# An attention and MLP kernel: a reordered prologue, warm-up matmuls, and unread matmuls in PE gaps

## The chip, the cores and the metric

The kernel runs on one core of one Trainium2 chip. The time is the device time of an execution in microseconds (us), lower is better. Three numbers recur: the *time* of an execution, the *span* of its profile (from the first to the last instruction, about 1.9 us shorter than the time), and the *ratio* to the kernel before.

Engines: PE is TensorE (PEld its weight loads), DVE is VectorE, ACT is ScalarE, POOL is GpSimd, SP is the engine that issues most of the DMAs. Lines of the profile name a source line as L640; L640 in the kernel before and L711 in the changed one are the same statement, an exponential on ScalarE.

## The reference

```python
xn = layernorm(A_x)                         # [1, 2048, 512]
# A: attention with 32 heads of 16 columns
qkv = xn @ wqkv
p = softmax(q @ k.T * 16**-0.5)             # 32 heads x 2048 x 2048
attn = (p @ v) @ wo
# B: a token-mixing MLP
h = layernorm(xn)
u = gelu(einsum("bsd,sf->bdf", h, w1) + b1) # F = 1376
mix = (einsum("bdf,fs->bds", u, w2) + b2).T
out = xn_input + attn + mix                 # xn_input is A_x
```

The heavy part is the softmax: 32 x 2048 x 2048 exponentials.

## The kernel before

A score tile has 128 keys, two heads and 512 queries, so it fills 128x1024 elements of PSUM. There are 1024 such tiles, in 32 blocks of 32. Each tile's exponential is done either by one ScalarE instruction or by VectorE with an integer approximation and three shifted copies. PE then multiplies the result with V ("pv").

```python
def score_specs(n):                       # two matmuls on two 32-row groups of the array
    ...
    fn=lambda e: e.matmul(bank(bk), lhsT=KT[32*r:32*r+32, T, 128*kt:128*(kt+1)],
                          rhs=QT[32*r:32*r+32, b % 4, :], start=True, stop=True,
                          tile_position=(32*r, 0)),
    reads=[("KTt", T, kt), ("QT", b % 4, r)], writes=[("bank", bk)]
def exp_specs(n):                         # ScalarE
    fn=lambda e: e.activation(buf(pbuf[n]), ps[:, s_*1024:(s_+1)*1024], ACTF.Exp, scale=LN2_128)
def dexp_spec(n, w):                      # the same tile on VectorE
    fn=lambda e: e.tensor_scalar(buf_i(w), ps[:, s_*1024:(s_+1)*1024], IBIAS, 0.0, ALU.add, ALU.max)
```

The program has three parts. In the *head*, x is loaded, four tiles of 128 tokens are normalised, transposed and projected to K, Q and V. In *block 0*, 32 score tiles are all done on ScalarE in a fixed order, while the remaining twelve token tiles are prepared in between. From block 1 on, a list scheduler inside the kernel orders everything by a cost model of its own while the program is built: the order is static, the semaphores come from declared reads and writes.

Each pair of blocks gets its Q rows by eight small copies on the DMA queue, and a score may be scheduled only when its Q block is marked as available:

```python
def score_has(n):
    b, kt, qb, G, T, e_ = blk_of(n)
    return ("q", b - b % 2) in have and ("k", T, kt // 4) in have
def task_qt(qb, T):
    ...                                   # project, scale, then eight row copies
    for e_ in range(2):
        slot = (8 * qb + 2 * T + e_) % 4
        for r in range(4):
            a = 32 * r + 16 * e_
            yield "sp", [dict(dst=QT[a:a+16, slot, :], src=Qall[a:a+16, :], ...)]
    yield "call", lambda: have.add(("q", 8 * qb + 2 * T))   # after all eight
```

A MLP or projection task (`cur_ext`) holds one PSUM bank, `EX_BANK`, for its accumulation.

The softmax here doesn't subtract the row's maximum and nothing guards it: scores larger than these inputs give would overflow.

## Time and profile before

| | before |
|---|---|
| time | 736.1 us, median of 3 (734.94 to 736.33) |
| first exponential on ScalarE starts | 15.69 us |
| last exponential ends | 726.50 us |
| exponentials on ScalarE / VectorE | 758 / 266 |
| ScalarE's waits on scores from 20 us on | 7.0 us |

The first useful view is the page's busy table (part 1), here of the kernel before:

```profile
span 734.8 us, 28211 instructions
PE 686.5 (93%) x12384; PEld 305.5 (42%) x12384; DVE 637.7 (87%) x1060; ACT 709.5 (97%) x780; POOL 350.1 (48%) x390
```

The second is the chain that ended last (part 4), by engine:

```profile
ACT 77%; PE 15%; DVE 4%; DMA 1%; POOL 1%; issue 0%; SPq 0%; DVEq 0%
```

Both say ScalarE. So the span is best read along ScalarE as three stretches: the *head* until the first exponential, the *body* from there to the end of the last one, and the *tail*. Only what shortens one of these moves the time.

Where does the body lose time? The next view is the timeline of ScalarE alone. Columns: start, length, engine, line, operation, shapes, count of merged instructions, and in brackets the idle time before them with what ended it. The lines shown are those with a bracket, from 15 to 51 us and from 505 to 508 us in the kernel before:

```profile
15.69 5.74 ACT L640 ACTIVATE pT<-ps 128x1024 bf16<-128x1024 f32 x6 [0.32 <-PE ps L616]
22.79 1.94 ACT L640 ACTIVATE pT<-ps 128x1024 bf16<-128x1024 f32 x2 [1.35 <-PE ps L616]
25.27 22.85 ACT L640 ACTIVATE pT<-ps 128x1024 bf16<-128x1024 f32 x24 [0.55 <-PE ps L616]
48.36 1.02 ACT L640 ACTIVATE x_sb<-ps 128x1024 bf16<-128x1024 f32 x1 [0.24 <-PE ps L616]
50.22 1.02 ACT L640 ACTIVATE x_sb<-ps 128x1024 bf16<-128x1024 f32 x1 [0.83 <-PE ps L616]
...
505.17 1.02 ACT L640 ACTIVATE pT<-ps 128x1024 bf16<-128x1024 f32 x1 [0.67 <-PE ps L616]
506.52 1.02 ACT L640 ACTIVATE pT<-ps 128x1024 bf16<-128x1024 f32 x1 [0.32 <-PE ps L616]
507.93 4.69 ACT L640 ACTIVATE pT<-ps 128x1024 bf16<-128x1024 f32 x5 [0.39 <-PE ps L616]
```

Every wait shown is for a score matmul (L616). The windows view says why PE was late there. Columns: stretch, its length, then busy time and instruction count of PE, PEld, DVE, ACT and POOL, then the granted clock of TensorE (1.00 is full speed), the DMA share and GB/s:

```profile
18.00:26.00 8.00, 7.28 (x68) 3.69 (x67) 5.96 (x19) 6.10 (x7) 3.27 (x8) 0.58 0.46 111
46.00:50.00 4.00, 3.65 (x32) 0.91 (x32) 1.49 (x2) 3.15 (x4) 3.80 (x3) 0.57 0.00 0
497.00:508.00 11.00, 9.92 (x110) 3.34 (x114) 8.95 (x16) 9.06 (x11) 5.23 (x5) 0.53 0.06 11
541.00:549.00 8.00, 6.95 (x76) 2.25 (x76) 7.13 (x12) 6.96 (x9) 4.18 (x4) 0.57 0.03 5
655.00:663.00 8.00, 7.26 (x96) 2.53 (x94) 6.40 (x9) 7.58 (x9) 3.13 (x3) 0.79 0.18 47
```

These are the stretches of halved clock. By the clock records of this trace they last 6.83, 3.41, 10.24, 6.83 and 3.41 us. ScalarE (the fourth pair of numbers) loses 0.4 to 1.9 us in each. The mean clock of the profile is 0.979.

### The profile page before, as it was taken

The numbers are of one execution on the slowest core, as the hardware profiler recorded it, in microseconds if no ns is written. First come the engines' busy times: TensorE is split into PE (matmuls) and PEld (weight loads), VectorE is DVE, ScalarE is ACT, GpSimd is POOL, SyncE is SP. The second block draws the span as 40 slices with busy tenths as digits, with TensorE's granted clock in tenths as the row PEclk, the third lists the DMA queues.
The fourth block names the chain that finished last, engine by engine and source line by source line (L and its number), as shares of the span: only waits on it lengthen the run. The fifth ranks groups of instructions, "written<-read, shape, count | busy, mean of one in ns | idle before, by whom it ended". The sixth has DMA issues, their size and how long they took to land.

```text
span 734.8 us, 28211 instructions
## 1 busy us (share of the span) xinstructions
PE 686.5 (93%) x12384; PEld 305.5 (42%) x12384; DVE 637.7 (87%) x1060; ACT 709.5 (97%) x780; POOL 350.1 (48%) x390
## 2 busy tenths in 40 slices
PE   4989999999999999999889999989989999999997
PEld 3434445444444444433334443433434444434442
DVE  6857788888898888898989999898999899989887
ACT  4899999999999999999999999998999999999995
POOL 5448455432433334445454544544555545645443
PEclk9899999999999999999999999997989999999999
DMA  7401000124232222220000212110000221221201
GB/s 201 94 2 25 18 9 21 25 59 89 44 70 62 41 66 59 57 49 18 22 21 20 52 37 67 38 32 12 20 17 18 49 49 39 50 50 41 46 22 44
DMA packets 85691, 32.25 MB, mean 44 GB/s; under 512 B 67392, under 2 KB 85568, under 8 KB 85568
## 3 DMA queue, kind: packets, MB, share of 16 engines
q1 hardware_dynamic: 82256, 28.74, 17.2%
q8 instruction: 97, 1.59, 0.9%
q10 hardware_dynamic: 3312, 1.70, 0.8%
q14 instruction: 26, 0.21, 0.1%
HBM read 21.76 MB, written 2.35 MB: 33 GB/s over the span
## 4 chain that ended last, share of the span: by engine, by line
ACT 77%; PE 15%; DVE 4%; DMA 1%; POOL 1%; issue 0%; SPq 0%; DVEq 0%
ACT pT L640 56%; ACT x_sb L640 21%; PE ps L616 5%; PE ps L679 5%; PE ps L709 4%; DVE pT L651 1%; DMA x_sb<-in_A_x_dram 1%; DMA wblk<-in_B_w_dram 1%; DVE pT L656 0%; DVE stats L452 0%; ACT ga_sb L812 0%; DVE x_sb L651 0%; POOL hx L478 0%; DVE x_sb L656 0%; DVE V L767 0%
## 5 line engine op out<-in xcount | busy, mean ns | idle before, releaser
L640 ACT ACTIVATE pT<-ps 128x1024 bf16<-128x1024 f32 x539 | 537.7, 1178 | 5.3 <-PE ps L616 5.1
L616 PE MATMUL ps<-QT,KT 32*128 32x512 bf16 x2048 | 285.3, 391 | 21.0 <-ACT pT L640 10.3
L651 DVE TENSOR_SCALAR pT<-ps 128x1024 int16<-128x1024 f32 x192 | 234.1, 1219 | 37.9 <-PE ps L616 36.9
L679 PE MATMUL ps<-pT,V 128*32 128x256 bf16 x4464 | 246.9, 281 | 6.1 <-DVE V L767 1.8
L640 ACT ACTIVATE x_sb<-ps 128x1024 bf16<-128x1024 f32 x219 | 240.9, 1171 | 2.3 <-PE ps L616 2.2
L656 POOL TENSOR_SCALAR pT<-pT 128x1024 int16<-128x1024 int16 x141 | 147.5, 1046 | 154.8 <-DVE pT L656 100.5
L616 PEld LDWEIGHTS ps<-QT,KT 32*128 32x128 bf16 x2048 | 79.2, 91 | 198.8 <-ACT pT L640 92.1
L679 PEld LDWEIGHTS ps<-pT,V 128*32 128x32 bf16 x4464 | 104.4, 96 | 110.3 <-issue 80.7
L679 PE MATMUL ps<-x_sb,V 128*32 128x256 bf16 x1760 | 115.3, 279 | 4.1 <-DVE OT L870 1.7
L656 DVE TENSOR_SCALAR pT<-pT 128x1024 int16<-128x1024 int16 x270 | 113.9, 443 | 2.7
L651 DVE TENSOR_SCALAR x_sb<-ps 128x1024 int16<-128x1024 f32 x74 | 90.1, 1218 | 12.4 <-PE ps L616 12.1
L656 POOL TENSOR_SCALAR x_sb<-pT 128x1024 int16<-128x1024 int16 x55 | 57.5, 1046 | 84.2 <-DVE pT L656 56.7
L656 POOL TENSOR_SCALAR pT<-x_sb 128x1024 int16<-128x1024 int16 x57 | 59.6, 1046 | 60.3 <-DVE pT L656 46.7
L679 PEld LDWEIGHTS ps<-x_sb,V 128*32 128x32 bf16 x1760 | 45.1, 96 | 41.8 <-issue 25.0
L679 PE MATMUL ps<-pT,VM 128*32 128x256 bf16 x764 | 55.2, 278 | 0.3 <-POOL VM L531 0.3
L709 PE MATMUL ps<-hx,wblk 128*32 128x512 bf16 x688 | 53.7, 381 | 1.5 <-DVE Qall L731 0.8
L656 DVE TENSOR_SCALAR x_sb<-pT 128x1024 int16<-128x1024 int16 x110 | 48.6, 446 | 1.1
L656 DVE TENSOR_SCALAR pT<-x_sb 128x1024 int16<-128x1024 int16 x108 | 43.9, 434 | 1.1
L709 PE MATMUL ps<-wkv_raw,wblk 128*32 128x512 bf16 x512 | 43.0, 381 | 1.8 <-DMA wblk<-in_B_w_dram 1.2
L907 POOL TENSOR_TENSOR oT<-oC,denb 128x256 bf16<-128x256 f32 (+1 forms) x32 | 23.3, 728 | 27.9 <-DVE pT L656 14.5
L679 PEld LDWEIGHTS ps<-pT,VM 128*32 128x32 bf16 x764 | 20.5, 97 | 9.0 <-issue 2.7
L656 POOL TENSOR_SCALAR x_sb<-x_sb 128x1024 int16<-128x1024 int16 x17 | 17.8, 1046 | 13.3 <-DVE pT L656 11.6
(89 smaller groups left out, 438.1 us busy)
## 6 DMA issues: line engine op xcount, KB each, us to landing
wblk<-in_B_w_dram SPq DMA_DIRECT2D x10, 512.0 KB, 4.6
wblk<-in_B_w_dram SPq DMA_DIRECT2D x16, 320.0 KB, 3.8
oC<-OT SPq DMA_DIRECT2D x248, 16.0 KB, 1.8
denb<-rden_scratch SPq DMA_DIRECT2D x124, 32.0 KB, 1.9
xr<-in_A_x_dram SPq DMA_DIRECT2D x16, 128.0 KB, 2.4
dcomp<-OT SPq DMA_DIRECT2D x124, 2.0 KB, 1.7
QT<-Qall SPq DMA_DIRECT2D x120, 16.0 KB, 1.8
out_dram<-osb SPq DMA_DIRECT2D x14, 128.0 KB, 1.9
```

The source lines that it names most:

```text
L616: specs.append(dict(eng="pe", fn=lambda e, r=r, bk=bk: e.matmul(bank(bk), lhsT=KT[32 * r:32 * r + 32, T, 128 * kt:128 * (kt + 1)], rhs=QT[ ...
L640: return [dict(eng="act", fn=lambda e: e.activation(buf(pbuf[n]), ps[:, s_ * 1024:(s_ + 1) * 1024], ACTF.Exp, scale=LN2_128), reads=[("ban ...
L651: return dict(eng="dve", fn=lambda e: e.tensor_scalar(buf_i(w), ps[:, s_ * 1024:(s_ + 1) * 1024], IBIAS, 0.0, ALU.add, ALU.max), reads=[(" ...
L656: return dict(eng=eng, fn=lambda e: e.tensor_scalar(buf_i(o), buf_i(w), float(SHIFTS[k]), 1.0, ALU.add, ALU.mult), reads=[("pT", w)], writ ...
L679: specs.append(dict(eng="pe", fn=lambda e, c=c, h=h, i=i, off=off: e.matmul(bank(PV_BANK)[32 * c:32 * c + 32, 256 * par:256 * par + 256], ...
L709: specs.append(dict(eng="pe", fn=lambda e, c=c, w=w: e.matmul(bank(EX_BANK)[32 * c:32 * c + w, :], lhsT=lhs_of(32 * c, 32 * c + w), rhs=rh ...
L907: yield "pool", [dict(eng="pool", fn=lambda e, cs=cs: e.tensor_tensor(oT[0:m, qb % 2, T, cs], oC32[0:m, tb_, cs], denb[0:m, tb_, cs], ALU. ...
```

## The change

Its intent: start the exponentials earlier, and keep TensorE's clock up, by matmuls whose results nobody reads. Four parts:

1. *Head*: x tiles 0 to 3 are loaded ahead of the weights on two queues; one tile's statistics go to ScalarE; the wo_t memset and the V projection leave the head; Q is evacuated in halves, V in pairs of tiles.
2. *Head warm-ups*: eleven matmuls of 512 columns before the first transpose.
3. *Block-0 warm-ups*: five at period 1, three each at periods 14 and 15.
4. *Fills*: from block 1 on, wherever the kernel's own model sees a gap of PE and little activity in the last 3.42 us, unread matmuls (the 3.42 us and the bound are constants chosen in the kernel, `ACT_WIN` and `ACT_MIN`).

Besides, many operations of the head get new cost figures in the scheduler's model.

The diff, cut to its core:

```diff
+N_WARM = 11
+ACT_WIN = 3.42
+ACT_MIN = 0.5
+    def pe_activity(self, t): ...        # modelled busy share of PE in the last ACT_WIN us
...
-        for j, a, b in (2,0,1),(1,0,1),(0,0,1),(1,1,4),(2,1,4),(0,1,4): ld_w on the ACT queue
-        ld_x(0, 1); ld_x(1, 2); ld_x(2, 4); ...                     # (shortened)
+        ld_x("sp", 0, 1); ld_x("act", 1, 2); ld_x("sp", 2, 3); ld_x("act", 3, 4)
+        for j in (1, 0, 2):
+            ld_w(j, 0, 1)
...
+        def warm_up(n, bk):
+            for _ in range(n):
+                sc.add("pe", lambda e: e.matmul(bank(bk), lhsT=warm[:, 0:128], rhs=warm, start=True, stop=True), ...)
+        ln_sums(1)
+        warm_up(N_WARM, 5)
...
+        for t in range(NPRE):
+            ln_norm(t)
+        late_memsets()                     # four memsets of VM on GpSimd
+        for t in range(NPRE):
+            transpose_pe(t, TB[t])
...
+            if period == 1:
+                warm_up(5, PV_BANK)
+            if period >= NKT - 2:
+                warm_up(3, 4)
...
+        def fill(t_next, same):
+            if cur_ext is not None or last_n is None or sc.pe_activity(t_next) > ACT_MIN:
+                return
+            ...
+            for _ in range(int((t_next - sc.pe_end - 2 * PE_SWITCH - 0.1) / 0.22)):
+                sc.add("pe", lambda e: e.matmul(bank(EX_BANK), lhsT=ident[:], rhs=wo_c[:, 0, :], ...), name="fill")
+            if kind in ("score", "pv", "ext"):
+                fill(t_est, kind == "score" and t_est <= sc.pe_end - 0.05)
```

## The prediction

5.3 + 2.5 + 2.8 = 10.6 us come off 736.1, which gives the 725.5.

> **What bounds the kernel now.** ScalarE. The page's busy table gives it 709.5 us of 734.8; the chain of waits that ended last is 77% ScalarE, nearly all exponentials. The groups view has 758 on ScalarE (539 + 219) and 266 on VectorE; back to back in the timeline, ScalarE starts one each 0.92 us, so 758 x 0.92 + 11 tanh x 0.5 is about 702 us that this change does not touch. The rest is a head of 15.7 us before the first exponential, about 8.5 us after the last, and idle time between (waits view from 20 us on: 7.0 us, all on score matmuls).
>
> Head (timeline): the first x tile's statistics are done at 3.97 us, but GpSimd is in a 1.8 us memset (wo_t) until 5.95, so its normalisation starts at 6.95; the third x tile lands only at 7.5, behind six weight loads on the other queue; PE runs at half speed until about 12.3 (0.61 us for four 128x128 matmuls, then 0.39).
>
> Idle time between (windows view): the granted clock is 0.50 in about 19.5-26, 46.5-50, 497-507.5, 541.5-548.5, and low around 655-662. ScalarE loses there 1.9, 1.1, 1.95, 1.1 and 0.3 us. [...] these stretches follow thin PE work (2-us windows with 6 to 10 matmuls at 496 and 540) and last multiples of about 3.4 us.
>
> **What changes.** Removed from the head: the wo_t memset, the V evacuations and half of the Q work before the first score; x tiles 0 to 3 now load ahead of the weights on two queues; one tile's sums go to ScalarE. Added: eleven 512-column warm-up matmuls (about 0.43 us each cold, 4.7 us, in idle time). Laid out with measured durations (statistics 0.69 + 0.18, power 0.57, normalise 0.4, transposes 0.4 warm, copy 0.6, evacuation 0.3 to 0.5): four normalised tiles at about 7.8 us, both Q halves and K tile 0 at about 9.9, first exponential at about 10.4. Gain 5.3 us, all on the chain (4 to 6.5).
>
> ScalarE stays the limit in block 0. Warm-ups at periods 1, 14 and 15 should save most of the 3.0 us lost around 20-26 and 46-50. I take 2.5.
>
> The unread matmuls land only in modelled gaps of over 0.5 us; I expect 100 to 400, PE busy up a little. They cost next to nothing: PE waits there for a score bank anyway. They save most of the 3.4 us lost around 500, 545 and 660: I take 2.8.
>
> The list schedule is computed anew, so the split of exponentials may move by a few either way: each is 0.92 us for ScalarE. I expect 755 to 761 on ScalarE; that is the widest term.
>
> **Prediction.** 736.1 - 5.3 - 2.5 - 2.8 = 725.5 or so: 725. Range 719 to 730. Faster by over 2% (below 721.4): 0.22; within 2%: 0.76; slower: 0.02.
>
> **Right or wrong would show as:** first exponential at 9.5 to 11.5 us in the timeline; no clock of 0.50 after the first exponential and a mean clock above 0.99; ScalarE's waits on scores from 20 us on below 2.5 us instead of 7.0; ScalarE busy total about the same within 4 us.
>
> **What would make it wrong:** weights landing late behind the x tiles, so that the first score waits for a DMA; fills that delay scores (a new wait on PE in full-array matmuls); clock drops that the model's activity does not see; VectorE falling behind in block 0; a different split.

## The result and the profile after

The median fell from 736.22 us (4 runs, 734.94 to 737.40) to 729.52 us (4 runs, 728.75 to 729.66): ratio 0.9907, 95% interval 0.9889 to 0.9925. The same changed kernel (the control e5 below) gave 730.20 and 0.9928. It was run at another time.

The page of the changed kernel, parts 1 and 4:

```profile
span 727.8 us, 28362 instructions
PE 690.1 (95%) x12448; PEld 307.5 (42%) x12459; DVE 636.5 (87%) x1060; ACT 706.9 (97%) x779; POOL 352.1 (48%) x390
ACT 70%; PE 20%; DVE 7%; POOL 1%; issue 1%; DMA 0%; DVEq 0%; ACTq 0%
```

ScalarE is as busy as before, within 2.6 us, but its share of the chain fell from 77% to 70% and PE's rose from 15% to 20%. Something on PE has become more of a limit than it was. ScalarE's timeline of the changed kernel, again the lines with a bracket from the first exponential to the last long wait, shows it:

```profile
11.25 3.77 ACT L711 ACTIVATE pT<-ps 128x1024 bf16<-128x1024 f32 x4 [0.48 <-PE ps L687]
15.40 26.87 ACT L711 ACTIVATE pT<-ps 128x1024 bf16<-128x1024 f32 x28 [0.38 <-PE ps L687]
245.18 1.02 ACT L711 ACTIVATE x_sb<-ps 128x1024 bf16<-128x1024 f32 x1 [0.53 <-PE ps L687]
256.95 1.02 ACT L711 ACTIVATE pT<-ps 128x1024 bf16<-128x1024 f32 x1 [0.20 <-PE ps L687]
258.51 1.02 ACT L711 ACTIVATE pT<-ps 128x1024 bf16<-128x1024 f32 x1 [0.53 <-PE ps L687]
302.87 3.77 ACT L711 ACTIVATE pT<-ps 128x1024 bf16<-128x1024 f32 x4 [3.75 <-PE ps L687]
```

The many waits around 22, 48, 505 and 545 us are gone. In their place stands one of 3.75 us at 302.87, longer than any wait for a score in the kernel before. Along ScalarE the profiles differ like this (the first two rows are read from the timeline, the tail is span minus the end of the last exponential):

| | before | after | difference |
|---|---|---|---|
| head: first exponential starts | 15.69 | 11.25 | -4.44 |
| body: first start to last end | 710.81 | 707.47 | -3.34 |
| tail | 8.30 | 9.08 | +0.78 |
| span | 734.8 | 727.8 | -7.0 |

The body's 3.34 us can be split further. One exponential fewer is on ScalarE (757 for 758), worth 0.92. The waits view from 20 us on has 5.2 us for 7.0: the old kinds of waits fell by about 5.5 us, from 7.0 to 1.5, and the new one put 3.75 back. The remaining 0.7 us is not in shorter waits: one of 0.38 us at 15.40 lies before the 20 us mark, and idle gaps under 0.15 us, which the view leaves out, rose from 0.3 to 0.6 us in all. It is in ScalarE's own busy time, which fell in the body from 703.5 to 701.2 us, 1.4 more than the one exponential explains. Counted in the trace, an exponential that starts after any idle time occupies ScalarE for 1.02 us, one that follows without a gap adds 0.92; there were 26 of the first kind and are 16. So each wait costs ScalarE about 0.1 us beyond its own length, here about 1.1 us together; the rest of the 1.4 is not traced further.

What was PE doing before 302.87? The chain in order of time (start, length, what) of the changed kernel:

```profile
298.71 2.08 PE ps L750 x76
300.78 1.73 PE ps L780 x32
302.51 0.54 PE ps L687 x6
```

PE was not idle and not slow. It worked through 76 pv matmuls and 32 of a projection (L780) before the next score (L687), because that is the program's order. The SP queue's timeline at the same place shows what the scheduler was holding the scores back for:

```profile
293.86 3.04 SPq L386 DMA_DIRECT2D QT<-Qall  x5
296.94 0.58 SPq L386 DMA_DIRECT2D denb<-rden_scratch  x1
297.57 2.03 SPq L386 DMA_DIRECT2D wblk<-in_B_w_dram  x2
...
301.76 2.73 SPq L386 DMA_DIRECT2D QT<-Qall  x3
```

Five of the eight row copies of a Q pair are issued at 293.86, then other transfers come in between, and the last three follow only at 301.76. The four that the waiting block needs are among the first five. But the scheduler releases the pair's scores only after the eighth.

### The profile page after: what moved, and what is told of

Its sections match the earlier page's. It is cut to its first block, busy times and chain, and to the rows that moved or that the text cites. A ratio compares the mean times of both kernels' runs of the same rounds, so it can differ in the third digit from the quotient of the medians.

```text
span 727.8 us, 28362 instructions
## 1 busy us (share of the span) xinstructions
PE 690.1 (95%) x12448; PEld 307.5 (42%) x12459; DVE 636.5 (87%) x1060; ACT 706.9 (97%) x779; POOL 352.1 (48%) x390
## 4 chain that ended last, share of the span: by engine, by line
ACT 70%; PE 20%; DVE 7%; POOL 1%; issue 1%; DMA 0%; DVEq 0%; ACTq 0%
ACT pT L711 50%; ACT x_sb L711 20%; PE ps L687 7%; PE ps L780 6%; PE ps L750 6%; DVE pT L722 3%; DVE pT L727 1%; DVE x_sb L722 1%; DVE x_sb L727 1%; DMA x_sb<-in_A_x_dram 0%; PE ps L595 0%; POOL pT L727 0%; ACT ga_sb L883 0%; PE ps L1030 0%; POOL mv L478 0%
## 5 line engine op out<-in xcount | busy, mean ns | idle before, releaser
L711 ACT ACTIVATE pT<-ps 128x1024 bf16<-128x1024 f32 x548 | 545.6, 1172 | 6.1 <-PE ps L687 5.6
L687 PE MATMUL ps<-QT,KT 32*128 32x512 bf16 x2048 | 283.8, 385 | 18.8 <-ACT pT L711 10.1
L722 DVE TENSOR_SCALAR pT<-ps 128x1024 int16<-128x1024 f32 x179 | 218.2, 1219 | 31.0 <-PE ps L687 30.2
L711 ACT ACTIVATE x_sb<-ps 128x1024 bf16<-128x1024 f32 x209 | 233.7, 1184 | 0.6 <-PE ps L687 0.5
L727 POOL TENSOR_SCALAR pT<-pT 128x1024 int16<-128x1024 int16 x133 | 138.9, 1045 | 145.7 <-DVE pT L727 97.8
L687 PEld LDWEIGHTS ps<-QT,KT 32*128 32x128 bf16 x2048 | 79.7, 91 | 192.8 <-ACT pT L711 83.8
L722 DVE TENSOR_SCALAR x_sb<-ps 128x1024 int16<-128x1024 f32 x88 | 107.4, 1220 | 16.8 <-PE ps L687 16.2
L727 DVE TENSOR_SCALAR pT<-pT 128x1024 int16<-128x1024 int16 x256 | 106.6, 442 | 2.2
L727 POOL TENSOR_SCALAR pT<-x_sb 128x1024 int16<-128x1024 int16 x63 | 65.8, 1045 | 70.0 <-DVE pT L727 57.8
L780 PE MATMUL ps<-hx,wblk 128*32 128x512 bf16 x688 | 54.9, 381 | 0.8 <-DVE u_sb L875 0.3
L727 DVE TENSOR_SCALAR pT<-x_sb 128x1024 int16<-128x1024 int16 x131 | 53.5, 437 | 1.3
L780 PE MATMUL ps<-wkv_raw,wblk 128*32 128x512 bf16 x512 | 43.8, 390 | 0.5 <-DVE osb L925 0.5
L727 DVE TENSOR_SCALAR x_sb<-pT 128x1024 int16<-128x1024 int16 x98 | 41.6, 436 | 0.8
L727 POOL TENSOR_SCALAR x_sb<-x_sb 128x1024 int16<-128x1024 int16 x25 | 26.1, 1045 | 31.4 <-DVE pT L727 21.3
L750 PEld LDWEIGHTS ps<-pT,VM 128*32 128x32 bf16 x796 | 21.1, 96 | 10.4 <-issue 4.5
```

What stands on the lines that cost most here:

```text
L687: specs.append(dict(eng="pe", fn=lambda e, r=r, bk=bk: e.matmul(bank(bk), lhsT=KT[32 * r:32 * r + 32, T, 128 * kt:128 * (kt + 1)], rhs=QT[ ...
L711: return [dict(eng="act", fn=lambda e: e.activation(buf(pbuf[n]), ps[:, s_ * 1024:(s_ + 1) * 1024], ACTF.Exp, scale=LN2_128), reads=[("ban ...
L722: return dict(eng="dve", fn=lambda e: e.tensor_scalar(buf_i(w), ps[:, s_ * 1024:(s_ + 1) * 1024], IBIAS, 0.0, ALU.add, ALU.max), reads=[(" ...
L727: return dict(eng=eng, fn=lambda e: e.tensor_scalar(buf_i(o), buf_i(w), float(SHIFTS[k]), 1.0, ALU.add, ALU.mult), reads=[("pT", w)], writ ...
L750: specs.append(dict(eng="pe", fn=lambda e, c=c, h=h, i=i, off=off: e.matmul(bank(PV_BANK)[32 * c:32 * c + 32, 256 * par:256 * par + 256], ...
L780: specs.append(dict(eng="pe", fn=lambda e, c=c, w=w: e.matmul(bank(EX_BANK)[32 * c:32 * c + w, :], lhsT=lhs_of(32 * c, 32 * c + w), rhs=rh ...
```

## The experiments

Two techniques keep the comparisons clean. The head and block 0 have a fixed order, so a change there shifts the rest without reordering it. And an unread matmul can be cut from 512 columns to 1 instead of being removed: order, semaphores and schedule stay the same, only its work is gone. The time that each kernel's own model gives is printed when it builds; it is used below only to say what was scheduled, not as a time. "Phase" means only whether the clock was first granted early or late in an execution.

| run | what | mean us | runs | ratio |
|---|---|---|---|---|
| after | the change | 729.36 | 4 | 0.9907 |
| e5_after_again | the change, control | 730.01 | 6 | 0.9928 |
| e1_qgate | + early release of Q blocks | 728.10 | 6 | 0.9902 |
| e2_fill1 | fills cut to 1 column | 732.47 | 6 | 0.9964 |
| e3_warmhead1 | head warm-ups cut to 1 column | 729.92 | 6 | 0.9929 |
| e4_warmbody1 | block-0 warm-ups cut to 1 column | 730.91 | 6 | 0.9943 |
| e6_h12 | two waits of the head removed | 729.40 | 6 | 0.9920 |
| e7_h3 | more head warm-ups | 728.07 | 5 | 0.9902 |
| e8_all | e1 + e6 + e7, no period-1 warm-ups | 725.78 | 5 | 0.9869 |
| e9_q3 | e1 + e7 | 726.05 | 5 | 0.9860 |
| e10_reorder | all unread matmuls cut to 1 column | 734.30 | 6 | 0.9972 |
| e11_beforefill | the kernel before + fills | 733.39 | 6 | 0.9961 |
| e12_all2b | e8, fills before a task starts, bound 0.55 | 726.18 | 5 | 0.9861 |

The runs e1 to e4 shared one chip, e5 to e8 a second, e9 to e12 a third; the runs of the kernel before, 11 in each, averaged 735.28, 735.36 and 736.28. All outputs were correct.

### e1_qgate: is the 3.75 us wait the lost gain?

My theory: the wait comes only from the release rule and costs its full length. Rival: PE has that work to do anyway and the wait moves.

```diff
-        return ("q", b - b % 2) in have and ...
+        return ("q", b) in have and ...
-            yield "call", lambda: have.add(("q", 8 * qb + 2 * T))         # after eight copies
+                yield "call", lambda e_=e_: have.add(("q", 8 * qb + 2 * T + e_))  # after each four
```

> The changed kernel, but a score may be scheduled as soon as the four row copies of its own Q block are queued, not all eight of the pair. My theory: the one new ScalarE wait of 3.75 us at 303 us comes only from the scheduler holding that block's scores back, so it vanishes and the time falls by 3 to 4 us, to about 726; 0.986 to 0.987 of the kernel before. Rival: the PE work at 299 to 303 us has to be done somewhere, and the wait only moves: within 1 us of 729.5 and other score waits of 3 us or more in its place.

Measured: 728.23 us median, 0.9902. The wait was gone from the profile, but the time fell by 1 to 2 us only, so on the time alone neither side was right. The profile showed where the rest went: the first exponential started at 12.62 instead of 11.25 us, with the same instructions in the head. One exponential more was on ScalarE (758), and a clock drop around 256 to 265 us took 1.7 us in waits. The body was 1.86 us shorter. The head's 1.4 us was a new question.

### e3_warmhead1 and e5_after_again: the head's warm-ups

```diff
         def warm_up(n, bk):
+            w = 1 if n == N_WARM else 512
             for _ in range(n):
-                ... e.matmul(bank(bk), lhsT=warm[:, 0:128], rhs=warm, start=True, stop=True)
+                ... e.matmul(bank(bk)[:, 0:w], lhsT=warm[:, 0:128], rhs=warm[:, 0:w], start=True, stop=True)
```

> The changed kernel in the same order, but the eleven warm-up matmuls ahead of the first transpose stream 1 column. Theory: the head's transposes and projections (about 54 matmuls of 128 columns between 6.7 and 10.8 us) then run at half speed for most of their length, and the first exponential starts 1 to 1.5 us later than 11.25; total 730.5 to 731. Rival: VectorE and GpSimd pace the head and PE only follows: first exponential within 0.3 us of 11.25 and the total unchanged.

> The changed kernel unaltered, as a control on the same chip as the next three. Theory: [...] in some executions the first exponential comes at 11.25 us, in others near 12.6, so the times should fall into groups about 1.4 us apart within 728.5 to 731. Rival: the spread is only noise of one group and the profile shows 11.25 again.

Without the warm-ups' work the first exponential came at 12.68 us, as my theory said. But the mean was 729.92 against 730.01 of the control: on average the eleven matmuls were worth nothing that shows above the noise (each is uncertain by about 0.4 us). The control's own profile has the first exponential at 12.51. PE's timeline of the head shows it; first the changed kernel as first profiled:

```profile
6.71 1.22 PE L526 MATMUL ps<-ident,hx 128*128 128x128 bf16 x12 [0.66 <-DVE hx L498]
8.54 0.40 PE L526 MATMUL ps<-ident,hx 128*128 128x128 bf16 x4 [0.61 <-DVE hx L498]
8.77 0.39 PE L577 MATMUL ps<-xnT,wq_sb 128*128 128x128 bf16 x4
9.22 0.83 PE L577 MATMUL ps<-xnT,wq_sb 128*128 128x128 bf16 x12
```

and the same kernel in the control:

```profile
1.17 4.26 PE L595 MATMUL ps<-osb 128*128 128x512 bf16 x11 [1.17 <-DVE b1c_bf L396]
6.77 1.21 PE L526 MATMUL ps<-ident,hx 128*128 128x128 bf16 x12 [1.34 <-DVE hx L498]
8.59 0.61 PE L526 MATMUL ps<-ident,hx 128*128 128x128 bf16 x4 [0.61 <-DVE hx L498]
8.99 0.63 PE L577 MATMUL ps<-xnT,wq_sb 128*128 128x128 bf16 x4
9.85 1.49 PE L577 MATMUL ps<-xnT,wq_sb 128*128 128x128 bf16 x12
```

Four transposes take 0.40 us in one and 0.61 in the other, twelve projections 0.83 and 1.49. In the control the clock was granted early: the eleven warm-ups took 4.26 us, while in the first profile they took 4.87. It was then withdrawn just ahead of the projections: the windows view gives the control a clock of 0.52 from 8 to 10 us and of 0.63 from 10 to 12, which is half speed from 8.1 to 11.5. (The windows view counts the time before the first clock record as 1.00, also where the durations say half speed: in e3 it reads 1.00 from 6 to 10 us, while four 128-column matmuls take 0.61 to 0.63 us there, against 0.39 to 0.40 in the first profile. So durations decide in the head.) The time of the first grant, read from the clock records, differs between the profiles. Three of the six profiles with eleven full warm-ups have the slow head: e5, e1 and e4, with the grant at 4.67, 4.89 and 4.89 us (their warm-ups took 4.26, 4.37 and 4.37 us) and a fall 3.4 us later, which lasted 3.4 us. In the three with the fast head (e6, the first profile, e2) the grant came at 5.11, 6.35 and 6.45 us (warm-ups of 4.48, 4.87 and 4.88 us) and nothing was withdrawn before 255 us. The slow head thus goes with an early grant in these six; why the grant comes earlier in one execution than in another is not shown. The expected groups are only partly visible in the control's times (727.94, then 730.10 to 731.10), because drops elsewhere overlap with them.

### e7_h3: warm-ups that hold

```diff
-N_WARM = 11
+N_WARM = 13
         for t in range(NPRE):
             transpose_pe(t, TB[t])
+            if t < NPRE - 1:
+                warm_up(1, 5)
```

> The changed kernel with 13 warm-ups instead of 11 and one more after each of the first three tiles' transposes. Theory: the clock no longer falls between the warm-ups and the projections in either phase, so no execution has its head matmuls at 0.61 to 0.63 us per four after 8.5 us: first exponential 11.3 to 11.9 in the profile, the slower group of executions disappears and the mean falls by 0.3 to 0.8 us. Rival: [...] the clock falls as before, and the extra warm-ups only delay: mean 0 to 0.8 us longer.

All five executions lay between 727.95 and 728.41 us and had a mean clock of 1.000, against 727.94 to 731.10 in the control. The mean fell by 1.94 us, more than expected, as no drop occurred in the body either. The drop at 256 us comes and goes as well. All twelve profiles of the changed kernel and its variants have one ScalarE wait of 0.53 us that ends between 244.7 and 248.5 us. In six of them the clock falls 10.3 to 11.0 us after its end (the changed kernel, e1, e2, e3, e5, e8); in the other six, e7 among them, it stays at 1.00 there. What decides between the two is not shown. So e7's five even executions may be in part luck: e9, with the same head, had a mean clock below 1.000 in three of five. PE's timeline of the head in e7:

```profile
6.69 0.40 PE L526 MATMUL ps<-ident,hx 128*128 128x128 bf16 x4 [0.29 <-DVE hx L498]
6.92 0.38 PE L595 MATMUL ps<-osb 128*128 128x512 bf16 x1
7.21 0.40 PE L526 MATMUL ps<-ident,hx 128*128 128x128 bf16 x4
7.45 0.38 PE L595 MATMUL ps<-osb 128*128 128x512 bf16 x1
...
9.23 0.83 PE L577 MATMUL ps<-xnT,wq_sb 128*128 128x128 bf16 x12
```

Its idle time before the first transpose is 0.29 us instead of the control's 1.34, and a warm-up matmul follows each of the first three tiles' transposes. None of the four profiles with this head (e7, e8, e9, e12) has slow projections (twelve take 0.83 us in e7 and e8), e9 included, where the grant came at 4.44 us by its clock record, earlier than in the three slow ones. In the control the clock fell across 16 transposes and two gaps (1.34 and 0.61 us); e7 put matmuls between the transposes and shortened the gaps to 0.29 and 0.28 us in one edit, so which of the two made the difference is not told apart here.

### e2_fill1: are the fills worth anything?

The changed kernel has 41 fills, all after 314 us. They were cut to 1 column.

```diff
-                    bank(EX_BANK), lhsT=KT[...], rhs=QT[32 * r:32 * r + 32, b % 4, :], ...
+                    bank(EX_BANK)[:, 0:1], lhsT=KT[...], rhs=QT[32 * r:32 * r + 32, b % 4, 0:1], ...
-                sc.add("pe", lambda e: e.matmul(bank(EX_BANK), lhsT=ident[:], rhs=wo_c[:, 0, :], ...
+                sc.add("pe", lambda e: e.matmul(bank(EX_BANK)[:, 0:1], lhsT=ident[:], rhs=wo_c[:, 0, 0:1], ...
```

> The changed kernel in the same instruction order, but the 41 unread matmuls of the fills stream 1 column instead of 512. Theory: the fills hold the clock up, so without their work two or three stretches of clock 0.50 return after 314 us, with 2 to 3.5 us of ScalarE waits on scores: about 732. Rival: the new schedule has no stretch thin enough, the 41 fills do nothing, and the time stays within 0.5 us of 729.5 with a clock of 1.00 after 314 us.

Measured: mean 732.47, ratio 0.9964 against 0.9928 for the control, about 2.5 us slower; and two executions of six ran slower still, up to 734.77 at a mean clock of 0.983. The windows view from 322 to 342 us, first e2:

```profile
322.00:342.00 20.00, 18.67 (x272) 7.80 (x272) 16.71 (x29) 18.06 (x21) 9.95 (x11) 0.74 0.06 15
```

then the changed kernel:

```profile
322.00:342.00 20.00, 18.63 (x313) 8.39 (x310) 18.02 (x31) 19.75 (x23) 10.98 (x12) 1.00 0.09 16
```

The clock is 0.74 in one and 1.00 in the other, and ScalarE works 18.06 us of 20 against 19.75. The order is the same, and the first grant came at about the same time (6.45 and 6.35 us), so this is the work of the unread matmuls and nothing else. The rival falls. But the place matters: this stretch, 327.3 to 337.5 us in the clock records, is none that the kernel before had. At its old places, around 500, 545 and 660 us, e2 keeps the full clock without the fills' work, for example:

```profile
500.00:510.00 10.00, 8.85 (x148) 3.50 (x144) 8.88 (x15) 10.00 (x12) 4.97 (x5) 1.00 0.09 24
540.00:550.00 10.00, 9.23 (x158) 4.18 (x158) 9.93 (x17) 10.00 (x13) 6.22 (x6) 1.00 0.13 26
```

e10's profile shows the same. In these executions the old stretches went with the new order of the program; whether a first grant at another time would bring them back is not shown. In three of e2's six the mean clock was lower (0.983 to 0.988) than in the profiled one (0.991); where those fell is not recorded.

### e4_warmbody1: the warm-ups of block 0

The same edit as in e3, for the groups of five and three.

> The changed kernel in the same order, but the warm-ups inside block 0 (five at period 1, three each at periods 14 and 15) stream 1 column. Theory: the five at period 1 delay a score by about 0.4 us, but without any of them the clock falls to 0.50 around 16 to 23 us or 42 to 46 us and ScalarE loses 1 to 3 us: 730.5 to 732. Rival: the block-0 warm-ups are not needed with the head's in place, no stretch of 0.50 appears before 50 us, and the time falls by 0.3 to 0.5 us to about 729.1.

Measured: mean 730.91, ratio 0.9943; against before it gains about 1.0 us less than the control, at the small end of my theory. In its profile the clock is 1.00 from 12 to 42 us and falls from 42 to 50 (0.61, 0.50, 0.50 and 0.68 in steps of 2 us), with waits of 0.49, 0.82 and 0.41 us; so the six at periods 14 and 15 are needed (e10's profile has the same stretch). The five at period 1 looked superfluous. That reading came from one profile, with its first grant at 4.89 us; e12 speaks against it.

### e6_h12: two waits of the head

In the changed kernel's timeline the fourth normalisation takes 0.87 us, and three GpSimd memsets run at the same moment:

```profile
7.61 0.87 DVE L498 TENSOR_SCALAR hx<-x_sb,mv 128x512 bf16<-128x512 bf16 x1
7.53 0.81 POOL L413 MEMSET VM<- 128x256 bf16 x3
```

The other three take 0.38 to 0.41. That the memsets hold up the fourth is my estimate from this coincidence, and e6 tests it by moving them. The second wait is one of bookkeeping: both halves of Q declare a write of the same key, so ScalarE's half waits 0.72 us for VectorE's.

```diff
-        late_memsets()                      # in the head
+            if period == 13:
+                late_memsets()
-        [("QT", 0, r) for r in range(4)]
+        [(("QT", 0, r) if half else ("QT0a", r)) for r in range(4)]
-        reads=[("KTt", T, kt), ("QT", b % 4, r)]
+        reads=[("KTt", T, kt), ("QT", b % 4, r)] + ([("QT0a", r)] if b == 0 else [])
```

> The changed kernel with two waits of the head taken away: GpSimd's four VM memsets moved from the head to period 13 of block 0, and the two halves of Q kept under separate keys so that ScalarE's half no longer waits for VectorE's. Nothing else in the order changes. Theory: the fourth normalisation takes 0.41 instead of 0.87 us [...], and the wait of 0.72 us before the ScalarE half of Q goes: first exponential 0.7 to 1.0 us earlier than the control at the same clock phase (about 10.4 where that has 11.25), total 0.7 to 1.0 us less. Rival: the K tiles' evacuation or the copies bind next and it gains under 0.3 us.

By the time it is inconclusive: mean 729.40 against 730.01, and both kernels have the lottery of the head's clock. The profile decides. The tile view of e6 (durations as minimum/median/maximum in ns):

```profile
L498 DVE TENSOR_SCALAR hx<-x_sb,mv x5: 380/407/414, 6.3 to 11.8; 128x512 bf16<-128x512 bf16 x5
```

No normalisation is slow any more (at most 0.414 us, with the memsets elsewhere), so the memsets beside it were the cause; by what mechanism is not shown. The first exponential starts at 10.74 us, 0.51 earlier than the 11.25 that the changed kernel has when its head runs at full speed. The only executions of this call with a mean clock of 1.000 differ by as much: 727.42 and 727.94; but one of the changed kernel in the first measurement took 728.75 at 1.000, so the times alone prove little. Expected were 0.7 to 1.0; ScalarE's half of Q now waits 0.52 us for the projections on PE, which bind next. What each of the two edits gave alone was not run.

### e9_q3: the first experiment without the lottery

The edits of e1 and e7 together.

> The changed kernel with the more robust head warm-ups (as in e7_h3) and the early release of Q blocks: the first experiment again, now without the lottery of the head's clock. Its schedule puts 758 exponentials on ScalarE against 757, so at equal waits it owes 0.9 us. Theory: against e7_h3 (728.0) the wait of 3.75 us goes and 0.9 us comes back: 725.2 to 725.8. Rival: the PE work of 299 to 303 us takes ScalarE's time elsewhere and the gain stays under 1 us: above 727.

Measured: 725.68 us median (724.97 to 727.14), ratio 0.9860. Against e7 in the profiles, at the same start of the first exponential (11.26), the body shrank from 706.22 to 703.50 us, by 2.7: 3.75 gained, 0.92 owed for the extra exponential, 2.8 expected. ScalarE's timeline of e9 at the old place:

```profile
295.79 2.08 ACT L713 ACTIVATE pT<-ps 128x1024 bf16<-128x1024 f32 x2
298.28 1.02 ACT L713 ACTIVATE pT<-ps 128x1024 bf16<-128x1024 f32 x1 [0.41 <-PE ps L689]
299.20 3.77 ACT L713 ACTIVATE x_sb<-ps 128x1024 bf16<-128x1024 f32 x4
302.81 2.90 ACT L713 ACTIVATE pT<-ps 128x1024 bf16<-128x1024 f32 x3
```

A wait of 0.41 us is left of 3.75, on a score that waits 0.18 us for one of its row copies. The rival of e1 falls: the work that PE did in the hole fits elsewhere. Two of its five executions had a mean clock of 0.995 and took about 727; the other three 725.0 to 725.7.

### e10_reorder: the order alone

The edits of e2, e3 and e4 together.

> The changed kernel in the same order with every unread matmul (warm-ups and fills) cut to 1 column: the new order of the head alone. Theory: the parts add: the fills were worth about 2.7 us, the warm-ups of block 0 about 0.7, those of the head 0.5 on average, so about 733 to 734 and 0.997 of before; two thirds of the gain of the change then hang on the unread matmuls. Rival: the order alone carries the gain, under 731.

Measured: mean 734.30, ratio 0.9972, as expected. The new order without its unread matmuls is worth 2.0 us, though its first exponential starts 3.15 us earlier than before (12.54), as the hole of 3.76 us is in it too. The parts add up: 2.0 for the order, about 2.5 for the fills (e2), 1.0 for the block-0 warm-ups (e4) and 0 for the head's (e3) make 5.5; the control has 5.35. Each term is uncertain by about 1 us, so the close agreement is partly luck (each is the difference to the mean of before, and for a cut, the control's 5.35 less the cut kernel's).

### e11_beforefill: fills on the kernel before

The fills' code copied into the kernel before, with one more condition: none after the last projection task, which leaves `EX_BANK` open for an accumulation.

> The kernel before with the fills alone (35 of them; none after the last projection, where the bank is kept open): old head, no warm-ups. The schedule puts 760 exponentials on ScalarE instead of 758, which costs 1.8 us. Theory: the stretches of clock 0.50 around 500, 545 and 660 us go, worth about 3 us, so the net is 0.5 to 1.5 us faster than before: 0.998 to 0.9985. Rival: fills are as good as they were in the changed kernel only with its other parts, and this one is slower than before by 1 us or more.

Measured: mean 733.39, ratio 0.9961, 2.9 us faster, which is more than expected. The new schedule has 760 exponentials on ScalarE instead of 758, so it owes 1.8 us, and still the body is 706.23 us against 710.81. With fills the old kernel gains without the other parts of the change. That the fills' work does it is not shown here, as they also made the scheduler order the program anew and no run cuts them to 1 column. The profile of this run lost less in block 0 too (one wait of 1.02 us instead of 1.35, 0.55, 0.24 and 0.83, in a part of the program that no fill touches, with the clock low there for 3.4 us instead of 10.2), so about 2 us of the body's 4.6 in this pair of profiles is the clock's luck.

### e8_all and e12_all2b: versions that beat both

e8 has the edits of e1, e6 and e7 and drops the five warm-ups of period 1. e12 adds fills while a task has not started its accumulation, raises `ACT_MIN` to 0.55, and stops the fills after the last projection as in e11.

> The changed kernel with the early release of Q blocks (as in the first experiment), both head waits removed, the extra head warm-ups, and without the five warm-ups of period 1. Theory: the gains add up: about 1.5 us of body from the first experiment, 0.8 us of head waits, 0.4 us at period 1, 0.4 us of head clock: 726 to 727, about 3 us under the control. Rival: without the warm-ups of period 1 the clock falls around 16 to 24 us and takes 1 us or more back.

> The combination e8_all with fills also while a task waits to start, and with the activity bound at 0.55 instead of 0.50 (57 fills instead of 30; 759 exponentials on ScalarE instead of 758). Theory: the remaining stretches of low clock around 256 and 324 us go (0.9 us of waits), the extra exponential takes 0.9 us: 725 to 726 with a smaller spread than e8_all and a clock above 0.998 in every run. Rival: denser fills delay scores: above 727.

e8: median 725.50 us (725.03 to 726.87), ratio 0.9869. e12: median 726.25 us (725.50 to 726.64), ratio 0.9861. Both lie about 4 us under the changed kernel. e12's theory was half right: its spread of 1.14 us is smaller than e8's 1.84, yet one run had a mean clock of 0.995, and its profile has the clock at 0.50 and 0.65 from 16 to 20 us with waits of 0.70 and 0.54 us there. That is the place where the five warm-ups of period 1 had been dropped, so dropping them on the word of e4 was probably a mistake: e7, which kept them and had its first grant at the same 5.75 us, has no drop there (1.00). e8, without them, had none either, with its first grant at 6.23 us; no run takes out these five alone. e9, which kept them and lacks the two head edits, is as fast as e8. A version with both was not run.

## Why the prediction was right or wrong

The prediction was 725 us with a range of 719 to 730. The first measurement, 729.52, lies just inside; the control's median, 730.20, just outside, so which side it fell on was luck. "Within 2%" was right. The centre was 4.5 us too low, and the runs say which terms did it.

- *ScalarE bounds the kernel.* Right: 97% busy before and after, and what moved its waits moved the time.
- *Head, gain 5.3 us, first exponential at about 10.4.* Mis-sized. 4.44 us in the first profile and 3.2 in the control. The term missed three things: 0.46 us that a normalisation lost beside GpSimd memsets (0.87 us, at most 0.41 in e6), the false dependence between the two halves of Q, and the clock. The prediction took the transposes and projections at full speed after the warm-ups ("0.4 warm"); in three of the six profiles with these warm-ups they ran at half speed (twelve projections in 1.49 us for 0.83), and the first exponential came 1.3 to 1.4 us later. Its worry, weights landing late, did not come true.
- *Warm-ups of block 0, 2.5 us, and fills, 2.8 us.* The sum was right, in part by luck: the old waits in the body fell by about 5.5 us. By the isolating runs, the fills gave 2.5 and the block-0 warm-ups 1.0; the rest came with the new order, as far as these profiles show. The step "They save most of the 3.4 us lost around 500, 545 and 660" failed: in the profiles of e2 and e10 those places keep a clock of 1.00 without the fills' work, and what the fills save is a stretch at 327 to 337 us that only the new order has. The size agreed with the 2.8 for another reason than the one given. The count was wrong: 41 fills, not 100 to 400.
- *"No clock of 0.50 after the first exponential."* Wrong. One drop remained around 256 us, where there is no fill (all 41 come after 314 us; most likely because a task is pending: e12, which relaxes this condition and the bound, has two fills at 254 us); it cost 0.74 us of waits in the profile, and it comes in six of twelve profiles (absent in e7).
- *"ScalarE's waits below 2.5 us."* Wrong: 5.2 us, of which 3.75 is the hole at 303 us. Here the step failed that says "The list schedule is computed anew, so the split of exponentials may move by a few either way ... that is the widest term". The split moved by one (757, as foreseen within 755 to 761). What moved was the order: the eight copies of one Q pair came apart on the DMA queue, and the release rule turned that into a hole on ScalarE. e9 shows its price, 3.75 us, and that it can be removed. The hole did not come with the fills, which all lie after 314 us, and it stays when their work is cut (3.76 us in e10); e11, with fills and the old head, has no such hole (its longest wait for a score is 1.02 us). So it came with the head's new order, or with the new cost figures that the diff gives the head's operations in the scheduler's model; these two were not told apart. Why the copies come apart there is not settled.
- *The tail*, for which the prediction allowed about the same 8.5 us, became 0.8 us longer (9.08). In the profile the last VectorE shifts end 0.8 us after the last exponential, against 0.1 us before it in the kernel before. It is 9.1 us in all the other profiles too, also in e11 with the old head, so it comes with the new schedules and not with the new head. No run isolates it.

Together: 10.6 us were promised. Short by 0.9 in the head (2.1 in the control), by 3.75 in the hole and by 0.8 in the tail; 0.9 came back with the exponential that moved to VectorE, 0.2 as the old waits fell a little more than foreseen, and 0.7 as ScalarE's busy time fell by 1.4 more while a wait at 15.40 and short gaps took 0.7 back. That is the 7.0 us of the spans. With the hole closed and the head's clock made firm, e9 measured 725.68 us, which is where the prediction stood.

## What to carry to other kernels

Matmuls whose results nobody reads can pay, when PE has slack and another engine waits for its latency (here about 2.5 us for 41 fills and 1.0 us for eleven in block 0); test them by cutting them to one column, which keeps the order. Look whether warm-up matmuls reach up to the work they are meant for: here, with gaps of 0.7 to 1.4 us in front of it, the clock fell ahead of the projections in three of six profiles and the first exponential came 1.3 to 1.4 us later in those, which a single profile does not show. When a change makes a scheduler order the program anew, look through the bottleneck engine's waits for a single new long one, and ask what rule held its producer back; and count each wait with the restart behind it, here 0.1 us. Here that one wait ate more than half of what the rest of the body had gained.
